# A Fourier mixing block and a gated feed-forward layer on one core: a new order for the first weights' conversions and loads

## The chip, the core and the metric

The kernel runs on one core of one Trainium2 chip. The time is the device time of the core in microseconds. Before the change it is 2035.06 us, the median of three runs (2034.91 to 2035.15). Engines are named as in the profile: PE (TensorE), DVE (VectorE), ACT (ScalarE), POOL (GpSimd) and SP, which only issues DMA transfers here.

## What is computed

The reference, cut to what matters, with x of 8 x 3008 x 256, `w_gate` and `w_val` of 256 x 1536 and `w_out` of 1536 x 256:

```python
X = np.fft.fft(np.fft.fft(x, axis=1), axis=2).real.astype(np.float32)
x = X.reshape(B * S, D)
gate = 1.0 / (1.0 + np.exp(-(x @ w_gate)))
val = x @ w_val
return (gate * val @ w_out).astype(np.float32)
```

`x` comes as float32. The three weights come as float64, 8 bytes a number, and the kernel turns them into float32 on the chip.

## The kernel before, in words

**Weights.** The 18 `jobs` are pieces of weights, 256 x 256 numbers each and 0.52 MB as float64: for each of six column blocks c one piece of the gate (w = 0) and one of the values (w = 1), and one of the output weights (w = 2), which comes one block later. In the order of the list: 0 and 1 are gate and value of block 0, 2 and 3 of block 1, 4 is output block 0, 5 and 6 gate and value of block 2, 7 output block 1, and so on to 17, output block 5. A piece goes through three stages. `weight_load` (L130) issues its DMA from SP into a place `raw`. The conversion is `weight_parts` (L161), two ACT operations (L166, L167), and `weight_join` (L169), three DVE operations (L176, L177, L179) and one POOL addition (L181). `weight_use` (L183) is a `merge` (L190) for gate and value: eight matmuls `ps` that fold the second Fourier transform (over the 256 features, table `dt`) into the weight, two ACT copies into `G2` and `G1` (L197, L198), and two small DMAs that turn one row of `G2` into the columns `ge` (L200). For the output weights it is `forms` (L203): two ACT copies and four POOL subtractions that make seven combinations in `wf`.

The places are borrowed from tiles that the main loop uses later: `raw` and `ws` of pieces 0 to 5 lie in tiles `z`, `pk`, `qk`, `ek`, `ae` and `h`; pieces 6 and 7 in the two tiles `c7`; the pieces from 8 on (`KEEP`) in one tile `mega` of the size of `x4`, which takes the place of the first sequence's input and so can be loaded only when that has been read for the last time.

**First Fourier transform.** Each of the 8 sequences is folded by its symmetries (`fold_ops`, L218), for sequence 0 in two halves on DVE and POOL at the start (L223 to L236), and then multiplied by tables of cosines and sines in `st`. The matmuls `ev` and `od` (`half`, L279) sum over six groups of rows; the four cosine groups of sequence 0 can start with half of the input and the first half of the cosine table, the two sine groups need the sine table. `then` copies one sum out with ACT (L291), and `places` adds and subtracts the other with DVE (L295, L298). The results are `pk`, `qk` and `ek`.

**Main loop.** A sequence's 1505 frequencies go in six chunks of up to 256, each against 12 blocks of 128 hidden features: 12 steps a chunk, 576 steps in all. Step i calls `front` (L343: matmuls `pa` and `pb`, on DVE two `ae` with a column of `ge`, and two `z`), `gate` for the step before (L365: one DVE product `h`, POOL sums `sf`), `back` for two pairs earlier (L388: six or eight matmuls `po`), the conversions' ACT part that is planned for this step (`pre`), the sigmoid (L573), and at last what `side` holds for the step: joins, loads, uses and other planned work. `at(i, f)` puts f into `side`. Every engine carries out its own instructions in the order in which the program gives them (a manual schedule), so a waiting instruction holds what stands behind it on its engine, and a waiting DMA issue holds all later issues of SP. The four PSUM tiles of `psx` are shared by `pa`, `pb`, `ps` and the sums.

**The order around the change.** At the start: loads 0 and 1, `x` of sequence 0, the cosine table, the sine table, loads 2 to 7. Then conversion 0 and merge 0, conversion 1 and merge 1, the fold and the cosine sums, the sine sums; conversions 2 to 5 stand one each ahead of the last four evacuations. `weight_use(2)` and loads 8 to 10 follow. In the first chunk, conversions 6 to 17 are planned by `weight_step` in the steps 1 to 8, two in the odd steps and one in the even ones, each one or two steps ahead of its use; the uses 3 to 17 stand in steps 0 to 9.

Of the kernel before, what the change touches and what calls it, by code (L numbers as in the profile page):

```python
# [7 lines left out]
F32 = mybir.dt.float32  # L8
I32 = mybir.dt.int32
# [36 lines left out]
def kernel(  # L46
# [11 lines left out]
    B, _, _, _, D = xf.shape  # L58
    F = moe_w_gate.shape[1]
    P = 128  # L60
# [6 lines left out]
    NPR = NFT // 2  # L67
    CH = 256
    WC = 256
# [9 lines left out]
    xp = ctx.enter_context(tc.tile_pool(name="xp", bufs=1))  # L79
    pqp = ctx.enter_context(tc.tile_pool(name="pqp", bufs=2))  # L80
    dram = ctx.enter_context(tc.tile_pool(name="dram", bufs=1, space=bass.MemoryType.DRAM))
    evp = ctx.enter_context(tc.tile_pool(name="evp", bufs=2))
    app = ctx.enter_context(tc.tile_pool(name="app", bufs=3))
    zp = ctx.enter_context(tc.tile_pool(name="zp", bufs=3))
    hp = ctx.enter_context(tc.tile_pool(name="hp", bufs=3))
    sp = ctx.enter_context(tc.tile_pool(name="sp", bufs=2))
    cp = ctx.enter_context(tc.tile_pool(name="cp", bufs=2))
    op = ctx.enter_context(tc.tile_pool(name="op", bufs=2))
# [14 lines left out]
    def load_x(b):  # L103
        X[b] = xp.tile([NP, 4, NQ, D], F32, name="x4", tag="x4")
        for h in range(0, 4, 2):
            nc.sync.dma_start(out=X[b][:, h : h + 2], in_=xf[b, :, h : h + 2])
# [11 lines left out]
    def load_table(t, nq):  # L118
        for q in range(0, NQ, nq):
            nc.sync.dma_start(out=st[:, t, q : q + nq], in_=stab[:, t, q : q + nq])  # L120
# [3 lines left out]
    jobs = [(w, c - (w == 2)) for c in range(NPR + 1) for w in range(3)  # L124
            if (c if w == 2 else c < NPR)]
    RAW, WS = {}, {}
    mega = []
    KEEP = 8

    def weight_load(j):  # L130


        w, c = jobs[j]
        src = (moe_w_gate, moe_w_val, moe_w_out)[w]
        src = src[2 * c * P : 2 * (c + 1) * P, :] if w == 2 else src[:, c * WC : (c + 1) * WC]
        src = src.rearrange("(c p) f -> p c f", p=P)
        if j < 6:
            if j < 3:
                raw = zp.tile([P, 2, WC, 2], I32, name="raw", tag="z")
            else:  # L140
                raw = pqp.tile([P, 2, WC, 2], I32, name="raw", tag=("pk", "qk", "ek")[j - 3])
            ws = (app if j < 3 else hp).tile([P, 2, WC], F32, name="ws", tag="ae" if j < 3 else "h")
        else:
            if j < KEEP:
                both = cp.tile([P, 3, 2 * WC], F32, name="both", tag="c7")
                r, i = 0, 2
            else:
                if not mega:
                    mega.append(xp.tile([P, 12, 2 * WC], F32, name="mega", tag="x4"))
                both, r, i = mega[0], (j - KEEP) % 3 * 2, 6 + (j - KEEP) % 6  # L150
            raw = both[:, r : r + 2].rearrange("p a n -> p (a n)").bitcast(I32).rearrange(
                "p (c f w) -> p c f w", c=2, w=2)
            ws = both[:, i].rearrange("p (c f) -> p c f", c=2)
        WS[j] = ws
        if src.dtype == F32:
            nc.sync.dma_start(out=ws, in_=src)
        else:
            RAW[j] = raw
            nc.sync.dma_start(out=raw.rearrange("p c f w -> p c (f w)"), in_=src.bitcast(I32))

    def weight_parts(j):  # L161

        if j in RAW:
            raw, ws = RAW[j], WS[j]
            lo, hi = raw[:, :, :, 0], raw[:, :, :, 1]
            nc.scalar.activation(ws, hi.bitcast(F32), AF.Abs)  # L166
            nc.scalar.activation(lo, lo.bitcast(U32), AF.Copy, scale=2.0 ** -29)  # L167

    def weight_join(j):  # L169
        if j not in RAW:  # L170
            return
        raw, ws = RAW.pop(j), WS[j]
        lo, hi = raw[:, :, :, 0], raw[:, :, :, 1]
        wi = ws.bitcast(I32)
        ts = nc.vector.tensor_scalar
        ts(out=ws, in0=ws, scalar1=2.0 ** -15, scalar2=HUGE, op0=ALU.max, op1=ALU.min)  # L176
        ts(out=wi, in0=wi, scalar1=3, scalar2=0x3FFFFFF8, op0=ALU.logical_shift_left,  # L177
           op1=ALU.bitwise_and)
        nc.vector.scalar_tensor_tensor(out=wi, in0=hi, scalar=-(2 ** 30), in1=wi,  # L179
                                       op0=ALU.bitwise_and, op1=ALU.bitwise_or)  # L180
        nc.gpsimd.tensor_tensor(wi, wi, lo, op=ALU.add)  # L181

    def weight_use(j, other=None):  # L183
        w, c = jobs[j]
        if w == 2:
            forms(WS.pop(j), c)
        else:
            merge(WS.pop(j), w, c, other)

    def merge(ws, g, c, other):  # L190
        cs = slice(c * WC, (c + 1) * WC)
        ps = bank("ps", other)
        for h in range(2):
            for t in range(2):
                mm(ps[:, h * WC : (h + 1) * WC], dt[:, t, h * HD : (h + 1) * HD], ws[:, t, :],
                   h == 0 and t == 0, t == 1)
        nc.scalar.copy(G2[:, g, cs], ps[:, WC : 2 * WC])  # L197
        nc.scalar.copy(G1[:, g, cs], ps[:, 0:WC])  # L198
        for f in range(c * WC // P, (c + 1) * WC // P):
            (nc.sync if c else nc.scalar).dma_start(  # L200
                out=ge[:, g, f : f + 1], in_=G2[0:1, g, f * P : (f + 1) * P])

    def forms(ws, c):  # L203

        w = ws.rearrange("p f (a h j) -> p f h a j", h=2, j=TB)
        f = wf[:, c].rearrange("p m (a j) -> p m a j", j=TB)
        sub = lambda o, a, b: nc.gpsimd.tensor_tensor(o, a, b, op=ALU.subtract)
        nc.scalar.copy(f[:, 0:2], w[:, :, 0])
        nc.scalar.copy(f[:, 2], w[:, 1, 1])
        sub(f[:, 4], w[:, 0, 1], w[:, 0, 0])  # L210
        sub(f[:, 6], w[:, 1, 1], w[:, 0, 1])
        sub(f[:, 5], w[:, 1, 1], f[:, 4])
        sub(f[:, 3], w[:, 1, 0], f[:, 5])
# [92 lines left out]
    def seq_start(b):  # L306
        PQE[b] = (pqp.tile([P, NK], F32, name="pk", tag="pk"),
                  pqp.tile([P, NK], F32, name="qk", tag="qk"),
                  pqp.tile([P, NK], F32, name="ek", tag="ek"))
        if b:  # L310
            nc.sync.dma_start(out=PQE[b][2], in_=ed[b - 1 : b, :].to_broadcast([P, NK]))

    def seq_group(b, blk, what, other=None):
        return half(lambda q: W[b, blk][what][:, q, :], PQE[b][what], blk, what == 1, P, other)
# [163 lines left out]
    for j in range(2):  # L478
        weight_load(j)
    load_x(0)  # L480
    load_table(0, NQ // 2)
    load_table(1, NQ)
    for j in range(2, KEEP):
        weight_load(j)
    for j in range(2):
        weight_parts(j)
        weight_join(j)
        weight_use(j)
    seq_start(0)
    cos = [seq_group(0, blk, what, (2 * blk, 2 * blk + 1) if what else None)  # L490
           for blk in range(2) for what in (0, 2)]
# [4 lines left out]
    sin = [seq_group(0, blk, 1) for blk in range(2)]  # L496
    for sums, _ in sin:
        sums(*range(NQ))
    cos[0][1]()()
    cos[1][1]()()  # L500
    for j, (_, then) in zip(range(2, 6), cos[2:] + sin):
        weight_parts(j)
        weight_join(j)
        then()()
    weight_use(2)
    for j in range(KEEP, KEEP + 3):
        weight_load(j)

    per = 2 * NPR * len(chunks)
    side = {}  # L510

    def at(i, *fs):
        side.setdefault(i, []).extend(fs)
# [2 lines left out]

        at(i, lambda: at(i + 1, f(*args)))

    def weight_step(i, *js):

        for j in js:
            pre.setdefault(i, []).append(lambda j=j: weight_parts(j))
            at(i, lambda j=j: weight_join(j))
            if KEEP <= j < len(jobs) - 3:
                at(i, lambda j=j: weight_load(j + 3))

    pre = {}
    for c in range(1, NPR + 1):
        i, j = 2 * c - 3, 3 * c - 1
        if c < NPR:  # L530
            if c > 1:
                at(i, lambda j=j: weight_use(j))
            at(i + 1, lambda j=j: weight_use(j + 1))
            at(i + 2, lambda j=j: weight_use(j + 2))
        else:
            at(i, lambda j=j: weight_use(j))
        if c == NPR:
            weight_step(i - 1, j)
        elif c > 1:
            weight_step(i - 1, *range(max(j, 6), j + 1))  # L540
            weight_step(i, j + 1, j + 2)
    i0 = 2 * NPR
    at(i0 + 1, lambda: load_x(1), e_load)

# [19 lines left out]
    for i in range(2 * len(pairs)):  # L564
# [7 lines left out]
        z = fresh[2]  # L572
# [63 lines left out]
```

## Time and profile before

| what | us |
|---|---|
| span of the profiled run | 2033.9 |
| busy: PE, DVE, POOL, ACT | 1998.4, 1754.1, 1334.9, 499.2 |
| first matmul of merge 0, of merge 1 | 8.96, 18.79 |
| first cosine sum, first sine sum | 24.41, 39.70 |
| first `pa` of steps 0, 1, 2, 3, 4 | 49.02, 52.47, 55.92, 65.30, 69.76 |
| first `pa` of steps 5, 6, 7, 8, 9 | 77.28, 83.27, 89.47, 95.44, 101.64 |
| idle of PE between 0 and 24.41 | 16.8 |
| idle of PE between 48 and 100 | 9.8 |

The page gives busy times as shares of the span; they are averages over a start, a first chunk with weights in it, and 560 steps without. Times in the text are counted from the start of the span. In a line of the timeline the first number is the start, the second the duration, and the bracket holds the idle time before it and what ended that. In the windows view, each row gives for one stretch the busy time of PE, PEld, DVE, ACT and POOL with the number of instructions, then the granted clock of PE, the share of time that the DMA engines were busy, and GB/s.

### The profile page before, as it was taken

Reading aid. Unit: us, or ns where it says so; the run is one execution under the profiler, and the core shown is the slowest. Engines: PE = TensorE matmul, PEld = TensorE weight load, DVE = VectorE, ACT = ScalarE, POOL = GpSimd, SP = SyncE. Lnnn points to the kernel's source line nnn. Section 1 sums busy time; section 2 is a strip of 40 time slices with the busy share of each in tenths; the row PEclk is TensorE's granted clock in tenths of the full one; section 3 lists DMA queues with packets and bytes.
Section 4 is the critical chain, followed back from the end, with each engine's and each line's share of the span. In section 5 each row is a group of like instructions: output and inputs, shape, how many; then the busy total and the mean of one; then the engine's idle time right before and its main releaser. Section 6 shows DMA issues by size and latency. Waiting matters only on the chain.

```text
span 2033.9 us, 27344 instructions
## 1 busy us (share of the span) xinstructions
PE 1998.4 (98%) x9168; PEld 1740.5 (86%) x9168; DVE 1754.1 (86%) x3221; ACT 499.2 (25%) x875; POOL 1334.9 (66%) x1675
## 2 busy tenths in 40 slices
PE   6899999999999999999999999999999999999998
PEld 4688789888998889888898888988889888898888
DVE  5999778987899878998889978899778988898887
ACT  2522222222222222222222222222222222222222
POOL 3779655875569745696457955589546875565665
PEclk9999999999999999999999999999999999999999
DMA  6340102010021000200011000201002010000001
GB/s 239 104 69 16 27 11 72 18 29 11 11 77 31 11 11 17 76 26 11 15 46 43 26 16 16 72 10 34 14 11 72 15 32 11 11 16 16 11 15 27
DMA packets 136176, 70.98 MB, mean 35 GB/s; under 512 B 127875, under 2 KB 128131, under 8 KB 133642
## 3 DMA queue, kind: packets, MB, share of 16 engines
q1 hardware_dynamic: 134214, 68.69, 12.3%
q8 instruction: 74, 1.21, 0.2%
q10 hardware_dynamic: 1822, 0.54, 0.1%
q14 instruction: 66, 0.54, 0.1%
HBM read 44.50 MB, written 24.68 MB: 34 GB/s over the span
## 4 chain that ended last, share of the span: by engine, by line
PE 86%; DVE 8%; POOL 4%; issue 1%; DMA 0%; ACT 0%; DVEq 0%; ACTq 0%; SPq 0%; POOLq 0%
PE po L93 37%; PE pa L93 21%; PE pb L93 21%; PE ev L93 3%; PE od L93 3%; DVE h L373 2%; DVE ae L358 2%; DVE z L362 1%; POOL x L233 1%; DVE z L361 1%; POOL x L231 1%; PE ps L93 1%; POOL sf L378 1%; DVE os L420 0%; POOL sf L377 0%
## 5 line engine op out<-in xcount | busy, mean ns | idle before, releaser
L573 ACT ACTIVATE z<-z 128x512 f32<-128x512 f32 (+1 forms) x576 | 358.5, 622 | 1311.4 <-DVE z L362 1311.3
L358 DVE SCALAR_TENSOR_TENSOR ae<-ek,ge,pa 128x256 f32<-128x256 f32 (+1 forms) x1152 | 489.8, 466 | 190.8 <-PE pa L93 188.1
L93 PE MATMUL pa<-pk,G 128*128 128x256 f32 (+1 forms) x2304 | 582.5, 375 | 0.0
L93 PE MATMUL pb<-qk,G 128*128 128x256 f32 (+1 forms) x2304 | 581.5, 375 | 0.0
L93 PE MATMUL po<-sf,wf 128*128 128x256 f32 (+1 forms) x2304 | 537.4, 375 | 1.4 <-POOL sf L378 0.7
L93 PEld LDWEIGHTS pa<-pk,G 128*128 128x128 f32 x2304 | 438.1, 190 | 57.2 <-issue 1.3
L93 PEld LDWEIGHTS po<-sf,wf 128*128 128x128 f32 x2304 | 436.2, 190 | 56.5 <-POOL sf L379 4.8
L93 PEld LDWEIGHTS pb<-qk,G 128*128 128x128 f32 x2304 | 438.0, 190 | 49.8
L377 POOL TENSOR_TENSOR sf<-h 128x256 f32<-128x256 f32 (+1 forms) x288 | 212.3, 737 | 391.4 <-DVE h L373 391.4
L373 DVE TENSOR_TENSOR h<-z 128x512 f32<-128x512 f32 (+1 forms) x576 | 453.3, 787 | 0.0
L361 DVE TENSOR_TENSOR z<-ae,pb 128x512 f32<-128x512 f32 (+1 forms) x576 | 390.1, 677 | 61.7 <-DVE ae L358 2.3
L93 PE MATMUL po<-h,wf 128*128 128x256 f32 (+1 forms) x1728 | 412.5, 375 | 0.0
L362 DVE TENSOR_TENSOR z<-ae,pb 128x512 f32<-128x512 f32 (+1 forms) x576 | 386.2, 670 | 0.0
L375 POOL TENSOR_TENSOR sf<-h 128x256 f32<-128x256 f32 (+1 forms) x288 | 220.2, 765 | 217.5 <-DVE h L373 212.6
L93 PEld LDWEIGHTS po<-h,wf 128*128 128x128 f32 x1728 | 328.3, 190 | 37.1
L378 POOL TENSOR_TENSOR sf<-sf,h 128x256 f32<-128x256 f32 (+1 forms) x288 | 216.2, 751 | 22.6
L379 POOL TENSOR_TENSOR sf<-h,sf 128x256 f32<-128x256 f32 (+1 forms) x288 | 214.3, 744 | 22.6
L460 ACT COPY c<-po 128x512 f32<-128x512 f32 (+1 forms) x141 | 76.9, 581 | 63.2 <-PE po L93 63.2
L420 DVE STREAM_TRANSPOSE os<-c 128x256 f32<-128x256 f32 x192 | 84.1, 438 | 0.2
L93 PE MATMUL ev<-st,x 126*128 126x377 f32 (+3 forms) x216 | 75.0, 479 | 1.8 <-DVE x L233 1.8
L93 PE MATMUL od<-st,x 126*128 126x377 f32 (+3 forms) x216 | 74.8, 478 | 0.0
L465 POOL TENSOR_TENSOR c<-c 128x512 f32<-128x512 f32 (+1 forms) x47 | 73.9, 1573 | 0.0
(83 smaller groups left out, 720.7 us busy)
## 6 DMA issues: line engine op xcount, KB each, us to landing
x<-in_xf_dram SPq DMA_DIRECT2D x16, 1512.0 KB
out_dram<-os SPq DMA_DIRECT2D x288, 64.0 KB
ek<-ed SPq DMA_DIRECT2D x7, 752.5 KB
out_dram<-os SPq DMA_DIRECT2D x92, 56.0 KB
st<-in_stab_dram SPq DMA_DIRECT2D x2, 1111.9 KB
st<-in_stab_dram SPq DMA_DIRECT2D x1, 2223.7 KB
mega<-in_moe_w_out_dram SPq DMA_DIRECT2D x4, 512.0 KB
raw<-in_moe_w_gate_dram SPq DMA_DIRECT2D x3, 512.0 KB
```

The source lines that it names most:

```text
L93: nc.tensor.matmul(o, l, r, start=start, stop=stop, skip_group_check=True)
L358: nc.vector.scalar_tensor_tensor(out=ae[:, g], in0=ek[:, ks], scalar=ge[:, g, f : f + 1], in1=pa[:, g], op0=ALU.mult, op1=ALU.add)
L361: nc.vector.tensor_tensor(z[:, :, 0], ae, pb, op=ALU.add)
L362: nc.vector.tensor_tensor(z[:, :, 1, ::-1], ae, pb, op=ALU.subtract)
L373: nc.vector.tensor_tensor(h[:, fh], z[:, 0], z[:, 1], op=ALU.mult)
L375: tt(s[:, 2], h[:, 0, 0], h[:, 0, 1], op=ALU.subtract)
L377: tt(s[:, 0], h[:, 0, 1], h[:, 1, 1], op=ALU.add)
L378: tt(s[:, 1], s[:, 0], h[:, 0, 0], op=ALU.subtract)
L379: tt(s[:, 3], h[:, 1, 0], s[:, 1], op=ALU.subtract)
L420: nc.vector.transpose(os_[:, s, 0:nb, h, :], t[:, slot, 0 : nb * TB])
L460: nc.scalar.copy(t[:, 2 * j : 2 * j + 2, 0:n], PO[j][:, :, 0:n])
L573: nc.scalar.activation(z[:, 0], z[:, 0], AF.Sigmoid)
```

## The change

Four edits. Conversions 0 and 1 both come ahead of merges 0 and 1. Loads 2 to 5 come ahead of the sine table. `KEEP` is 10 in place of 8: pieces 6 and 7 get their `raw` in the tiles `os`, 8 and 9 in the tiles `sf`, and their results in the tiles `c7`. Conversions 2 to 8 are spread over the six evacuations, and those from 9 on stand one a step in steps 0 to 8, with load j+3 behind conversion j. The uses keep their steps, but for the last, which moves from step 9 to step 11. It is to let the first sums start earlier, and to keep merges from waiting for conversions.

```diff
-    KEEP = 8
+    KEEP = 10
...
+        if j < KEEP:
+            pool, tag = ((zp, "z"), (pqp, ("pk", "qk", "ek")[j % 3]), (op, "os"), (sp, "sf"))[
+                j // 3 if j < 6 else j // 2 - 1]
+            raw = pool.tile([P, 2, WC, 2], I32, name="raw", tag=tag)
...
+                ws = some(3, cp, "c7")[:, (j - 6) % 3].rearrange("p (c f) -> p c f", c=2)
...
     load_x(0)
     load_table(0, NQ // 2)
+    for j in range(2, 6):
+        weight_load(j)
     load_table(1, NQ)
-    for j in range(2, KEEP):
+    for j in range(6, KEEP):
         weight_load(j)
-    for j in range(2):
-        weight_parts(j)
-        weight_join(j)
-        weight_use(j)
...
+    weight_parts(0)
+    weight_parts(1)
+    weight_join(0)
+    weight_join(1)
+    weight_use(0)
+    weight_use(1)
...
-    cos[0][1]()()
-    cos[1][1]()()
-    for j, (_, then) in zip(range(2, 6), cos[2:] + sin):
-        weight_parts(j)
-        weight_join(j)
+    evacuate = [then for _, then in cos + sin]
+    for then, js in zip(evacuate, ((2, 3, 4), (5,), (), (), (6, 7), (8,))):
+        weight_round(*js)
         then()()
-    weight_use(2)
     for j in range(KEEP, KEEP + 3):
         weight_load(j)
+    weight_use(2)
...
-        if c == NPR:
-            weight_step(i - 1, j)
-        elif c > 1:
-            weight_step(i - 1, *range(max(j, 6), j + 1))
-            weight_step(i, j + 1, j + 2)
+    for j in range(9, len(jobs)):
+        pre.setdefault(j - 9, []).append(lambda j=j: weight_parts(j))
+        at(j - 9, lambda j=j: weight_join(j))
+        if KEEP <= j < len(jobs) - 3:
+            at(j - 9, lambda j=j: weight_load(j + 3))
+    for j in range(3, len(jobs)):
+        w, c = jobs[j]
+        at(2 * c + (-3, -2, 1)[w], lambda j=j: weight_use(j))
```

More of the change, by code (lines that the diff above doesn't have):

```diff
@@ L126 @@
     RAW, WS = {}, {}
-    mega = []
-    KEEP = 8
+    shared = {}
+    KEEP = 10
     def weight_load(j):
@@ L136, in weight_load, with some @@
         src = src.rearrange("(c p) f -> p c f", p=P)
-        if j < 6:
-            if j < 3:
-                raw = zp.tile([P, 2, WC, 2], I32, name="raw", tag="z")
-            else:
-                raw = pqp.tile([P, 2, WC, 2], I32, name="raw", tag=("pk", "qk", "ek")[j - 3])
-            ws = (app if j < 3 else hp).tile([P, 2, WC], F32, name="ws", tag="ae" if j < 3 else "h")
-        else:
[L144 to L150, printed above, removed]
+        def some(n, pool, tag):
+            key = tag, (j - 6) // 3 if tag == "c7" else 0
+            if key not in shared:
+                shared[key] = pool.tile([P, n, 2 * WC], F32, name=f"w{tag}", tag=tag)
+            return shared[key]
+        if j < KEEP:
+            pool, tag = ((zp, "z"), (pqp, ("pk", "qk", "ek")[j % 3]), (op, "os"), (sp, "sf"))[
+                j // 3 if j < 6 else j // 2 - 1]
+            raw = pool.tile([P, 2, WC, 2], I32, name="raw", tag=tag)
+            if j < 6:
+                pool, tag = ((app, "ae"), (hp, "h"))[j // 3]
+                ws = pool.tile([P, 2, WC], F32, name="ws", tag=tag)
+            else:
+                ws = some(3, cp, "c7")[:, (j - 6) % 3].rearrange("p (c f) -> p c f", c=2)
+        else:
+            both = some(12, xp, "x4")
+            r, i = (j - KEEP) % 3 * 2, 6 + (j - KEEP) % 6
             raw = both[:, r : r + 2].rearrange("p a n -> p (a n)").bitcast(I32).rearrange(
@@ L481, with weight_round @@
     load_table(0, NQ // 2)
+    for j in range(2, 6):
+        weight_load(j)
     load_table(1, NQ)
-    for j in range(2, KEEP):
+    for j in range(6, KEEP):
         weight_load(j)
-    for j in range(2):
-        weight_parts(j)
-        weight_join(j)
-        weight_use(j)
+    def weight_round(*js):
+        for j in js:
+            weight_parts(j)
+            weight_join(j)
+    weight_parts(0)
[4 more added lines that the diff above has]
+    weight_use(1)
     seq_start(0)
@@ L517, in split @@
         at(i, lambda: at(i + 1, f(*args)))
[L519 to L525, printed above, removed]
-    pre = {}
[L528 to L536, printed above, removed]
-        if c == NPR:
-            weight_step(i - 1, j)
-        elif c > 1:
-            weight_step(i - 1, *range(max(j, 6), j + 1))
-            weight_step(i, j + 1, j + 2)
+    pre = {}
+    for j in range(9, len(jobs)):
[6 more added lines that the diff above has]
+        at(2 * c + (-3, -2, 1)[w], lambda j=j: weight_use(j))
     i0 = 2 * NPR
```

## The prediction

> **What bounds the kernel now.** First the page: busy time by engine, and the chain of waits.
>
> ```profile
> PE 1998.4 (98%) x9168; PEld 1740.5 (86%) x9168; DVE 1754.1 (86%) x3221; ACT 499.2 (25%) x875; POOL 1334.9 (66%) x1675
> ...
> PE 86%; DVE 8%; POOL 4%; issue 1%; DMA 0%; ACT 0%; DVEq 0%; ACTq 0%; SPq 0%; POOLq 0%
> ```
>
> TensorE (PE) is busy 1998.4 of 2033.9 us, so all that any reordering can win is 35.5 us of PE idle plus matmuls that ran slowly. Next, PE's waits in three stretches (before 48 us, 48 to 100, after 100) say where that idle time is.
>
> ```profile
> PE ps L93 <- POOL ws L181: 15.0, 2, 9.0
> PE ev L93 <- DVE x L233: 1.8, 1, 1.8
> ...
> PE ps L93 <- POOL mega L181: 5.9, 5, 2.5
> PE ps L93 <- POOL both L181: 3.9, 1, 3.9
> ...
> PE ps L93 <- POOL mega L181: 1.2, 1, 1.2
> PE po L93 <- POOL sf L378: 0.7, 3, 0.3
> ```
>
> 16.8 us lie in the start, 9.8 in the first chunk, 1.9 later; the rest is the tail. Everything but the 1.8 and the 0.7 is a merge (`ps`) waiting for the last operation of a weight conversion (L181). From 101.64 us on PE runs without a break, so what the change moves is the time at which that begins. The timeline of the start:
>
> ```profile
> 8.96 3.78 PE L93 MATMUL ps<-ws,dt 128*128 128x256 f32 x8 [8.96 <-POOL ws L181]
> ...
> 14.43 0.66 ACT L166 ACTIVATE ws<-raw 128x512 f32<-128x512 f32 x1 [1.00 <-ACT G L198]
> ...
> 15.13 0.40 SPq L159 DMA_DIRECT2D raw<-in_moe_w_gate_dram  x1
> ...
> 18.79 3.78 PE L93 MATMUL ps<-ws,dt 128*128 128x256 f32 x8 [6.04 <-POOL ws L181]
> ...
> 24.41 1.53 PE L93 MATMUL ev<-st,x 126*128 126x377 f32 x4 [1.83 <-DVE x L233]
> ```
>
> Conversion 1 starts on ScalarE (ACT) at 14.43, behind merge 0's copies; VectorE's (DVE) fold waits in DVE's order behind it until 16.65, and the first cosine sum behind the fold until 24.41. Then the first chunk by windows (PE, PEld, DVE, ACT, POOL busy, PE clock, DMA share, GB/s):
>
> ```profile
> 57.80:61.70 3.90, 0.01 (x1) 0.00 (x0) 3.73 (x7) 2.06 (x6) 3.82 (x6) 0.85 0.03 0
> 61.70:66.30 4.60, 4.57 (x11) 3.68 (x12) 4.04 (x6) 1.39 (x4) 3.81 (x4) 0.50 0.00 0
> ...
> 72.90:101.60 28.70, 22.76 (x101) 18.76 (x101) 27.73 (x46) 14.04 (x29) 24.15 (x26) 1.00 0.38 111
> ```
>
> From 72.90 to 101.60 DVE is busy 27.73 of 28.70 us and PE only 22.76: **DVE bounds the first chunk**, because twelve conversions share steps 1 to 8 with the chunk's own DVE work. At 61.70 PE also runs at half clock after an idle 3.9 us.
>
> **What the Trainium skill says.** "TensorE: Matmul & The Clock Gate", Part 1, says that an idle window of about 3.4 us halves the clock until about 3.4 us of work have passed. The trace agrees: after 3.91 us idle the eight `ps` matmuls took 3.78 us, after 2.51 us idle only 1.99. "SBUF — State Buffer", Who interferes with whom, says that a DVE instruction with two SBUF inputs, or in a two-port mode, and a GpSimd (POOL) instruction block each other. The trace agrees: L223 took 0.94 us alone and 2.03 with POOL busy, L177 0.43 and 0.84. "DMA: Bandwidth & Descriptors", Anatomy of one DMA, says that a semaphore wait is held by the issuing sequencer. The trace agrees: SP's issue of weight 2 stood 9.0 us for a landing of `x`, and the loads queued after it stood too.
>
> **The change part by part.**
>
> *First two conversions together.* Nothing is removed; ACT no longer puts merge 0's copies (12.78) before conversion 1. Until 15 us the windows sum to 0.5 MB by 4.0 us and 1.34 MB by 6.0, so weight 1 (0.52 MB after weight 0 and the 0.26 MB table) is there at about 6.4. ACT then ends both at 7.7, DVE at about 9.1, POOL at 10.5. Merge 1 follows merge 0 at 12.74 and ends near 15 instead of 22.57. The fold no longer waits for the conversion but for `x`: its first half (4.2 MB cumulative less 1.5) at about 10.6, the second at 15.1 (the issue released at 15.13 waited for it). From L223 at 21.16 to L233's end at 24.36 the chain takes 3.2 us; POOL's 2.52+0.98 us of folding, now at the same time, cost DVE some 2 more (in the trace 16.87 to 21.22 cost it 1.1+1.5). First cosine at 15.1+3.2+2 = 20.3, 4.1 us earlier. But PE has then idled 5 us, so its first 4.5 us go at half clock: 2.2 us back. Cosines (15.1 us) end at 37.6, sines (7.6) at 45.2, DVE's last `qk` 1.1 later: **46.3 instead of 48.56, −2.2 us**.
>
> *Four loads ahead of the sine table.* 2.1 MB go before the table. Cumulative: 6.7 MB up to the cosine table, 8.8 with the four, 11.1 with the sine table; the windows of before reach 11.1 MB at 33.6 us. The table is wanted at 37.6. So it is hidden, unless SP stands: before, weights 3 and 4 waited until 21.26 and 27.56 for `ge` landings. If the table is issued only at 27.6 and 1 MB of weights with it, it lands at 27.6+3.3/0.4+1 = 37; still on time.
>
> *Seven instead of four conversions before the steps.* They move 3 conversions of DVE work into a stage that has DVE idle: 5.2 us in 30 to 40, 1.8 in 40 to 50. Seven at 1.55 (0.43+0.43+0.69) to 2.0 (with the 0.89 form) is 10.9 to 14.0 us, plus six evacuations of 1.09 = 6.5. From the fold's end (29.94 before, about 25.4 after): 25.4+17.4 to 20.5 = 42.8 to 45.9, under the 46.3 above. So they cost nothing there: the sines hide them. The ten places only make this possible.
>
> *One conversion a step, nine in steps 0 to 8.* Their DVE time, from the timeline: 0.41+0.83+1.10 = 2.34 us alone, 2.07 to 2.09 as one of a pair; I take 2.2. The chunk's own DVE work is 0.87+0.69+0.60+0.60 = 2.73 a step. Check on before: 9 steps of `ae`, `z` (19.4) and 8 of `h` (5.2) with 12 conversions (25.7) are 50.3 us, against 49.3 busy between 48.56 and 103.9. After: 24.6+9×2.2 = 44.4 us, 5 less. Idle before was 6.0 us in that stretch: 4.1 for `pa` at the start, after the half clock, and after merges that PE held up while waiting for POOL. Each weight is now converted two to four steps before its use, so those waits go, and with them the half clock. At steps 0 and 1 a conversion fills the gap. I keep 2 us. PE itself needs 9×1.72 (`pa`, `pb`) +5×1.51 (`po`) +9×1.73 (merges) = 38.6 us, less than DVE's, so it doesn't bound.
>
> *A new wait on SP.* The loads of steps 1 to 5 now come before that step's `ge` transfers in SP's order, and wait for POOL's L181 of the same step. Behind them stand the `ge` rows of merges 6 and 9, needed two steps on by `ae` on DVE. From a step's DVE begin: join ends at 5, POOL 6.8, two issues to 7.9, the load's 0.5 MB 1.3 to 2, landing near 11 (before: 2.0 to 2.5 from issue to landing); the need is at 10.2. Not shown by the trace of before; bounds 0 and 2×2 us, I take 1.5. The odd steps have a step more of slack.
>
> First chunk: 44.4+2+1.5 = 47.9 against 55.3, **−7.4**; I shorten it to −6.9, for PE and DVE are close (4.96 and 4.93 a step) once `po` runs. Later work has the same instructions; the last form moves from step 9 to 11, before the load of `x` at step 13. Sum: −2.2−6.9 = −9.1, 2035.1−9.1 = **2026.0 us**.
>
> **The rivals.** *A, both parts in full:* the start keeps its 4.1 us (clock warm) and no `ge` wait: −4.1−8.9 = −13, **2022 us**. For it: merge 1 ends just 5 us before the cosine, and the clock's window is coarse. *B, one part is lost:* no start gain (−6.9), or `ge` stalls of 1.5 us at four even steps, 6 us in place of 1.5 (−4.6): about −5, **2030 us**. For it: SP's longest wait for a `ge` landing was 5.9 us. Against: the windows then had DMA share 0.9, in the chunk 0.38. *C, slower:* the sine table's issue waits for the second pair of `ge` rows. The first pair took 6.3 us apart (21.26, 27.56); at that pace the second pair lands at 34 and 40. Table at 40+2.3/0.4+1 = 46.7, sines to 54.3, `qk` at 55.4, +6.8; weights 6 to 9 land later still and put ACT behind, so that the chunk gains 3, not 7: +4, **2039 us**. Against: 20 us of idle DMA would then shorten those landings.
>
> **How the numbers follow.** Forecast 0.50, A 0.22, B 0.20, C 0.05, 0.03 for none of these within 0.2%. 0.2% is 4.1 us, so faster ends at 2031.0: forecast, A and nearly all of B less a part that falls within, 0.90; same 0.05; slower 0.05. The range takes in A with the unknown waits at nothing (2020.5) and B up to 2031.5.
>
> **What would show it.** Right: `ev` starts at 20 to 21 us, sines end at 44 to 46, no `ps` wait for L181 between 50 and 100, step 9 begins near 92, DVE above 94% busy from step 1 to 8, the tail unchanged in length. Wrong: PE waiting for `st` between 35 and 48 (table late), DVE idle before `ae` for `ge` at steps 4 and 6, or the half clock again inside the chunk.

## The result, and the profile after

| | before | changed |
|---|---|---|
| median of six runs, us | 2035.11 (2034.75 to 2036.59) | 2029.43 (2024.31 to 2032.67) |
| ratio, with 95% interval | | 0.9968 (0.9955 to 0.9982) |
| span of the profiled run, us | 2033.9 | 2028.5 |
| first cosine | 24.41 | 23.85 |
| first `pa` of step 0 | 49.02 | 54.92 |
| first `pa` of step 9 | 101.64 | 96.87 |

The changed kernel is faster by 0.32%, and its times spread over 8.4 us where those of before spread over 1.8. The page of the changed kernel, busy time by engine and the chain of waits:

```profile
PE 1996.6 (98%) x9168; PEld 1743.3 (86%) x9168; DVE 1754.9 (87%) x3221; ACT 498.5 (25%) x875; POOL 1328.4 (65%) x1675
...
PE 85%; DVE 7%; POOL 4%; DMA 2%; issue 1%; ACT 0%; DVEq 0%; SPq 0%; ACTq 0%; POOLq 0%
```

The work is the same. DMA, which had 0% of the chain, now has 2%. PE's waits before 48 us, from 48 to 110, and after:

```profile
PE ev L93 <- DMA st<-in_stab_dram: 11.7, 2, 8.8
PE ps L93 <- POOL ws L187: 9.3, 1, 9.3
...
PE pb L93 <- DVE ae L364: 2.5, 3, 1.5
...
PE po L93 <- POOL sf L384: 0.2, 1, 0.2
```

No merge waits for a conversion any more but the first. (Lines have moved: L176, L177, L179 and L181 of the conversion are L182, L183, L185 and L187, the `ae` of L358 is L364.) In its place PE waits for the tables in `st`. So the whole gain is in the first chunk, and the start lost: from the start of the span to step 0 the changed kernel took 5.9 us more, and steps 0 to 9 took 41.95 us instead of 52.62, 10.7 less; the rest, 0.6 less, makes the 5.4 us between the spans. The start by its timeline:

```profile
9.35 5.76 PE L93 MATMUL ps<-ws,dt 128*128 128x256 f32 x16 [9.35 <-POOL ws L187]
...
18.60 0.95 DVE L229 TENSOR_TENSOR x<-x 126x765 f32<-126x765 f32 x1 [4.26 <-DMA x<-in_xf_dram]
...
22.85 0.56 DVE L239 TENSOR_TENSOR x<-x 126x381 f32<-126x381 f32 x1
...
23.85 2.85 PE L93 MATMUL ev<-st,x 126*128 126x377 f32 x4 [8.75 <-DMA st<-in_stab_dram]
...
29.38 0.46 SPq L120 DMA_DIRECT2D st<-in_stab_dram  x1
...
43.84 3.73 PE L93 MATMUL ev<-st,x 126*128 126x377 f32 x6 [2.92 <-DMA st<-in_stab_dram]
```

Both merges run one after the other and end at 15.1 us, as planned. But the second half of `x` is there only at 18.60, and the part of the fold that PE needs ends at 23.41. PE starts at 23.85, after 8.75 us of standing; what came last for it was not the fold but the first half of the cosine table. The sine table, issued at 29.38, holds PE from 40.9 to 43.84, and the six matmuls after it take 3.73 us, where six at full clock take 2.06: the half clock, a second time. The same stretches of both kernels in the windows view, the changed kernel first:

```profile
12.00:20.00 8.00, 3.10 (x11) 2.24 (x9) 3.31 (x5) 1.29 (x4) 1.53 (x2) 1.00 0.95 295
20.00:28.00 8.00, 4.15 (x8) 2.44 (x9) 7.77 (x13) 0.00 (x0) 2.96 (x3) 0.57 0.92 250
28.00:36.00 8.00, 8.00 (x26) 4.74 (x25) 6.17 (x9) 5.63 (x10) 5.11 (x6) 1.00 0.91 297
```

and the kernel before:

```profile
12.00:20.00 8.00, 1.96 (x5) 1.05 (x5) 4.81 (x6) 1.87 (x4) 3.13 (x2) 0.76 0.94 362
20.00:28.00 8.00, 6.17 (x19) 3.68 (x18) 7.78 (x15) 0.65 (x2) 2.81 (x3) 0.81 0.92 324
28.00:36.00 8.00, 8.00 (x27) 4.81 (x26) 2.95 (x3) 1.64 (x4) 3.73 (x4) 1.00 1.00 365
```

The last two columns are to be seen: the DMA engines were as busy (0.91 to 0.95 against 0.92 to 1.00) but moved 250 to 297 GB/s in place of 324 to 365. The first chunk, steps 0 to 9, of the changed kernel, and then of the kernel before:

```profile
54.70:96.60 41.90, 39.38 (x179) 33.53 (x178) 37.42 (x63) 23.15 (x53) 26.19 (x32) 1.00 0.34 100
```

```profile
48.80:101.40 52.60, 42.75 (x179) 35.29 (x178) 46.98 (x77) 28.51 (x60) 37.18 (x41) 0.94 0.34 101
```

The same 179 matmuls, with 63 DVE instructions instead of 77, 9.6 us less DVE work, and a clock of 1.00 instead of 0.94. Not all of the 9.6 us is saved: some of it only falls after the stretch, because PE is further ahead of DVE at its end than it was before.

### The profile page after: what moved, and what is told of

Its sections match the earlier page's. It is cut to its first block, busy times and chain, and to the rows that moved or that the text cites. A ratio compares the mean times of both kernels' runs of the same rounds, so it can differ in the third digit from the quotient of the medians.

```text
span 2028.5 us, 27347 instructions
## 1 busy us (share of the span) xinstructions
PE 1996.6 (98%) x9168; PEld 1743.3 (86%) x9168; DVE 1754.9 (87%) x3221; ACT 498.5 (25%) x875; POOL 1328.4 (65%) x1675
## 4 chain that ended last, share of the span: by engine, by line
PE 85%; DVE 7%; POOL 4%; DMA 2%; issue 1%; ACT 0%; DVEq 0%; SPq 0%; ACTq 0%; POOLq 0%
PE po L93 37%; PE pa L93 21%; PE pb L93 21%; PE ev L93 3%; PE od L93 3%; DVE ae L364 2%; DVE h L379 2%; DVE z L368 1%; DMA ge<-G 1%; DVE z L367 1%; POOL x L239 1%; POOL x L237 1%; DMA st<-in_stab_dram 1%; POOL sf L384 1%; POOL sf L383 1%
## 5 line engine op out<-in xcount | busy, mean ns | idle before, releaser
L364 DVE SCALAR_TENSOR_TENSOR ae<-ek,ge,pa 128x256 f32<-128x256 f32 (+1 forms) x1152 | 489.7, 466 | 186.1 <-PE pa L93 181.9
```

The source lines that it names most:

```text
L364: nc.vector.scalar_tensor_tensor(out=ae[:, g], in0=ek[:, ks], scalar=ge[:, g, f : f + 1], in1=pa[:, g], op0=ALU.mult, op1=ALU.add)
```

## The experiments

The times of all runs, with the ratio to the kernel before on the same chip and points of the profiled run. Not all rows are from one chip, so it is the ratio that compares them. `qk` is the end of the last DVE operation that makes it.

| run | median us | ratio (95%) | first cosine | `qk` | step 0 | steps 0 to 9 |
|---|---|---|---|---|---|---|
| before_again | 2036.67 | | 25.1 | 51.0 | 51.4 | 51.4 |
| after_again | 2030.79 | 0.9970 (0.9959 to 0.9982) | 23.3 | 53.6 | 54.0 | 42.0 |
| ge_sync | 2029.61 | 0.9971 (0.9958 to 0.9984) | 24.5 | 52.7 | 52.5 | 41.8 |
| table_first | 2029.71 | 0.9968 (0.9956 to 0.9981) | 21.2 | 54.5 | 50.0 | 45.2 |
| merge_first | 2030.29 | 0.9968 (0.9956 to 0.9980) | 25.1 | 53.7 | 54.2 | 41.9 |
| old_start | 2033.20 | 0.9982 (0.9967 to 0.9997) | 24.7 | 54.0 | 50.7 | 44.1 |
| skip_678 | 2029.15 | 0.9961 (0.9947 to 0.9974) | 24.2 | 52.5 | 52.9 | 42.0 |
| split_joins | 2028.87 | 0.9960 (0.9947 to 0.9972) | 25.5 | 54.4 | 54.2 | 40.2 |
| no_table | 2026.58 | 0.9950 (0.9936 to 0.9964) | 24.5 | 51.3 | 51.5 | 42.0 |
| two_ahead | 2031.69 | 0.9977 (0.9968 to 0.9985) | 25.3 | 59.2 | 53.6 | 47.1 |
| chunk_pairs | 2032.01 | 0.9976 (0.9967 to 0.9986) | 24.6 | 54.7 | 54.4 | 43.4 |
| eleven_in_chunk | 2035.84 | 0.9995 (0.9986 to 1.0003) | 25.4 | 54.9 | 54.9 | 47.0 |

From step 9's `pa` to the last `po`, all of these runs and the first two took 1924 to 1926 us, so that the differences lie before step 9. The intervals of the ratios are some 2.5 us to either side: only differences beyond that are settled by the times alone.

**Both kernels once more** (`before_again`, `after_again`). No edit.

> The kernel before, for a second profile. Theory T (in the changed kernel the start now hangs on transfers: x until 18.6 us, the sine table until 43.8): here the transfers are hidden behind merge 1 and the cosines, so whether the DMA moves 350 to 380 GB/s between 12 and 20 us (as in its first profile) or 240 to 300 (as in the profile of the changed kernel), the first cosine starts at 24 to 25.5, step 0 at 49 to 50.5, and the time is 2034.5 to 2037. Rival N (the DMA is slow only because of the changed order): always 350 to 380 GB/s here.

> The changed kernel once more. Theory T: its time follows the DMA's rate in the start: with 350 GB/s or more between 12 and 20 us the first cosine starts at 20 to 21.5, PE waits less than 1 us for the sine table, and the run takes 2026 or less; with under 300 it starts at 23 to 25, PE waits 2 us or more for the table, and it takes 2029 or more. The spread over runs is 5 us or more where that of before is 2. Rival D (DVE's seven conversions set the end of the sines): the spread is not tied to the table, and DVE is busy throughout from 31 to 53 us.

The kernel before, in its second profile, in windows:

```profile
12.00:20.00 8.00, 1.96 (x5) 1.12 (x4) 4.12 (x5) 1.87 (x4) 2.44 (x2) 1.00 0.89 312
20.00:28.00 8.00, 5.94 (x14) 3.71 (x13) 7.81 (x15) 0.65 (x2) 2.85 (x2) 0.88 1.01 296
```

Here the old order moves 312 and 296 GB/s, not 362 and 324, so rival N falls: the rate is in part a matter of the run. Step 0 was 2.4 us later than in the first profile, 0.9 more than T allowed; the time is among those of before on that chip (2035.4 to 2038.1). So the loss at the start depends on the pair of profiles: step 0 of the changed kernel is 5.9 us later in the first pair, 2.6 in this one (54.0 against 51.4), and its steps 0 to 9 are 10.7 and 9.4 us shorter. The changed kernel went by T's branch for a low rate (301 GB/s, a little above T's 300; first cosine at 23.3, 2.7 us of waiting for the table, 2029.7 in that run). Its spread was only 2.5 us, so the spread of 8.4 in the first set was not seen here; that point of T was missed.

**Sine table ahead again** (`table_first`).

```diff
-    for j in range(2, 6):
-        weight_load(j)
     load_table(1, NQ)
-    for j in range(6, KEEP):
+    for j in range(2, KEEP):
         weight_load(j)
```

> The sine table goes ahead of loads 2 to 5 again (this part of the change undone), the rest stays. Theory T: the table lands before 36 us and PE never waits for it; but weights 2 to 4 land 4 to 6 us later and stand on ACT ahead of the evacuation of the first cosine sum, whose PSUM tile the first sine needs, so PE waits there for 0 to 4 us instead; step 0 begins at 47 to 52 against 54.9, the time is 2022 to 2028. Rival D: step 0 not before 54, the time within 1 us of the changed kernel's.

PE's waits before 60 us:

```profile
PE pb L93 <- DVE qk L301: 3.1, 1, 3.1
PE od L93 <- DVE pk L304: 1.6, 1, 1.6
```

The table was never waited for, and step 0's `pa` came at 50.0, as T had it. But weight 2 reached DVE only after DVE had stood 7.7 us, the conversions ran until 53.6, and `pb` waited 3.1 us for `qk`. The evacuation of the first cosine behind weight 4 cost PE 1.6 us, as T had it, `qk` at 54.5 is what D had. The time is that of the changed kernel: T's 2022 to 2028 was missed, D's was right. Before the steps both have to arrive early, the table for PE and the weights for DVE.

**The ge transfers of merges 0 and 1 off the path of the loads** (`ge_sync`).

```diff
-            (nc.sync if c else nc.scalar).dma_start(
+            nc.sync.dma_start(
                 out=ge[:, g, f : f + 1], in_=G2[0:1, g, f * P : (f + 1) * P])
```

> The four ge transfers of merges 0 and 1 are issued by SP behind load 9 instead of by ACT, so that no load at the start waits for their landing. Theory T: loads 4 and 5 and the sine table are issued by 20 us instead of 25.9 to 29.4, the dip of the DMA between 28 and 31 us goes, the table lands 2 to 4 us earlier, and the time falls by 2 to 4 us against the changed kernel (to about 2026). Rival D: the table lands earlier, and the time stays within 1 us.

PE had no wait for the table here, and the dip went (383 GB/s from 28 to 31 us, against 213 in the changed kernel). Step 0 came 1.5 to 2.4 us earlier. The median is 1.2 us lower and the ratio the same, so no gain in the time is shown. SP's own timeline, and the first sine:

```profile
7.27 8.49 SPq L165 DMA_DIRECT2D raw<-in_moe_w_gate_dram  x1
15.80 6.25 SPq L120 DMA_DIRECT2D st<-in_stab_dram  x1
...
43.11 2.14 PE L93 MATMUL ev<-st,x 126*128 126x377 f32 x6
```

The second number is how long the issue itself took, 8.49 and 6.25 us instead of the 0.37 to 0.47 of most others: with some seven transfers under way, an issue stood although nothing that the profile shows was waited for. Loads 4 and 5 were out by 15.8 us, the table only at 22.05. Even so, its issue began 13.6 us earlier than in the changed kernel, and the table did not land earlier: its last landing event in the trace is at 43.02, against 43.70 and 42.81 in the changed kernel's two profiles. T's 2 to 4 us are missed, and a late issue is not what makes the table late. PE came to the sines 2.2 us later than in the changed kernel (first cosine at 24.5, and a longer half clock), so it stood no time before them, and took them at full clock (2.14 us for six matmuls instead of 3.73). That is where step 0 gained.

**The first edit undone alone** (`merge_first`). Conversion 0, merge 0, conversion 1, merge 1, as before.

```diff
-    weight_parts(0)
-    weight_parts(1)
-    weight_join(0)
-    weight_join(1)
-    weight_use(0)
-    weight_use(1)
+    for j in range(2):
+        weight_round(j)
+        weight_use(j)
```

> Only the first edit undone: conversion 1 comes after merge 0 again. Theory T2: with x landing at 17 to 19 us the conversion of weight 1 (over at 16.7) hides in the wait for x, so the first cosine starts within 1.5 us of the changed kernel's 23.3 to 23.9, PE is warmer there (it has just done merge 1), and the time is within 1 us. The prediction's view (the edit brings the first cosine 4.1 us forward): 2 to 4 us slower than the changed kernel.

T2 was right: first cosine 25.1 instead of 23.3 to 23.9, but at full clock, because merge 1 has just been done (the wait before it is 1.8 us); step 0 at 54.2 against 54.0 to 54.9; the same time. The edit that was forecast at 2.2 us shows no gain here. Nor could one show: PE stood before the sines in this run too.

```profile
PE ev L93 <- ACT a L297: 2.5, 1, 2.5
```

The wait is put down to an evacuation, which ended at 43.05; the sine table's last landing event is at 42.92, so without the evacuation PE would have started only 0.1 us sooner.

**Both edits of the start undone** (`old_start`). The diffs of `table_first` and `merge_first` together.

> The changed kernel with both edits of the start undone (conversion 0, merge 0, conversion 1, merge 1; sine table ahead of loads 2 to 5), so seven conversions at the start and one a step remain. Theory T2 (the chunk's new order wins about 10 us of its own, and the start of the change costs because PE gets the table late and DVE its weights late): the first cosine starts at 24 to 25.5, DVE has weight 2 only at 33 or later and is then busy to the end of the start, step 0's pb at 54 to 57, steps 0 to 9 take 41 to 44 us against 51.4 to 52.6 before; the time is 0 to 3 us above the changed kernel's. Rival S (the edits of the start are what is lost, without them all is better): step 0 at 49 to 51 as before, the time 3 to 6 us below the changed kernel's.

DVE waited 11.3 us for weights, weight 2 came at 33.9, `pb` of step 0 at 53.55, steps 0 to 9 took 44.1 us, and the median was 2.4 us above the changed kernel's: near T2 in each number (`pb` came 0.4 us before its range, the steps took 0.1 us more). Rival S's 3 to 6 us less are not in the median. But the intervals overlap, the six times run from 2028.3 to 2038.1 us, and the profile is of the lowest, below the changed kernel's own profile (2028.3 against 2029.7). So this run doesn't settle which start is better, given seven conversions in it.

**Less DVE work at the start** (`skip_678`). As ge_sync, without L182 and L183 of conversions 6 to 8.

```diff
-        ts(out=ws, in0=ws, scalar1=2.0 ** -15, scalar2=HUGE, op0=ALU.max, op1=ALU.min)
...
+        if not 6 <= j <= 8:
+            ts(out=ws, in0=ws, scalar1=2.0 ** -15, scalar2=HUGE, op0=ALU.max, op1=ALU.min)
```

> As ge_sync, but the two tensor_scalar operations of conversions 6, 7 and 8 are left out, so those three pieces of the weights are wrong; it takes 3.3 to 4 us of DVE work out of the start (0.42+0.43, 0.42+1.40, 0.80+0.43). Theory T2 (once the table is no longer late, DVE's conversions set the end of the start): step 0's pb 2.5 to 4 us earlier than in ge_sync (52.9 there), and the time 2 to 4 us below it. If transfers or PE set the end of the start: step 0 and the time within 1 us of ge_sync.

T2 missed: step 0 at 52.9 against 52.5, with the first cosine at 24.2 against 24.5. PE's last sum ended at 51.35 and `qk` 1.1 us later, as soon as DVE can; in ge_sync `qk` came 1.8 us after the sum. So the conversions hold the start up by 0.7 us at most when the weights come in this order. T2's condition, a table no longer late, was not met: PE stood 1.8 us before the sines, with no releaser named in the profile, and started at 43.52, when the table's last landing event (43.43) had come. The times don't settle it alone (medians 0.5 us apart, ratios 0.0010).

**No sine table** (`no_table`). From here on theory X: transfers bind the start.

```diff
-    load_table(1, NQ)
...
-                mm((ev, od)[q % 2], w(q), st[:, int(sn), q, c0 : c0 + n], q < 2, q >= NQ - 2)
+                mm((ev, od)[q % 2], w(q), st[:, 0, q, c0 : c0 + n], q < 2, q >= NQ - 2)
```

> The changed kernel without the load of the sine table (2.28 MB); the sines are taken with the cosine table, so the transform's sine part is wrong, the work on the engines the same. Theory X (with skip_678 missed, the start is bound by transfers: x sets the first cosine, the bytes ahead of the table's end set the sines): no gap and no second half clock of PE near 41 us, sines from 40.5 to 48.5, step 0 at 49.5 to 51.5 instead of 53.8 to 54.7, time 2.5 to 4.5 us below the changed kernel. Rival D (DVE's conversions hold the last qk anyway): step 0's pb not before 53, time within 1.5 us.

PE's waits in this run, up to 130 us:

```profile
PE ev L93 <- DMA st<-in_stab_dram: 10.0, 1, 10.0
PE ps L93 <- POOL ws L187: 9.4, 1, 9.4
PE pb L93 <- DVE ae L364: 2.6, 3, 1.5
```

The wait at 41 us is gone, the one ahead of the first cosine is left, and the small ones of the chunk. Step 0 at 51.5 and 4.2 us less time than the changed kernel are X's; the sines, from 42.2 to 49.9, were 1.4 to 1.7 us later than X had them, and it is the cosine table and not `x` that the profile names for the first cosine. So the table's bytes, with the half clock that they bring, are worth 2.5 to 3.4 us at step 0. The landing events say the same of every kernel here that has loads ahead of the sine table:

| run | last landing of the sine table | first sine |
|---|---|---|
| changed kernel | 43.70 | 43.84 |
| after_again | 42.81 | 42.94 |
| ge_sync | 43.02 | 43.11 |
| merge_first | 42.92 | 43.05 |
| skip_678 | 43.43 | 43.52 |
| split_joins | 44.70 | 44.79 |
| two_ahead | 44.11 | 44.20 |
| chunk_pairs | 44.86 | 45.00 |
| eleven_in_chunk | 45.38 | 45.52 |

Each time the sines begin 0.09 to 0.14 us after the table's last landing, whatever else was changed.

**Two loads ahead of the table in place of four** (`two_ahead`). With ge_sync's edit, and the loads of the chunk behind that step's `ge`.

```diff
-    for j in range(2, 6):
+    for j in range(2, 4):
         weight_load(j)
     load_table(1, NQ)
-    for j in range(6, KEEP):
+    for j in range(4, KEEP):
...
-((2, 3, 4), (5,), (), (), (6, 7), (8,))
+((2, 3), (), (), (4, 5), (6, 7), (8,))
```

> A version meant to be better, from theory X: ge of merges 0 and 1 on SP, in the chunk the loads behind that step's ge transfers, and only loads 2 and 3 ahead of the sine table, 4 and 5 behind it, with the conversions spread (2, 3), none, none, (4, 5), (6, 7), (8) over the evacuations. Theory X: the table lands 1.05 MB, 3 to 3.5 us, earlier than in ge_sync, PE has no gap at 40, step 0 at 50.5 to 52.5, steps 0 to 9 in 40 to 41 us (no ge waits), time 2025 to 2028. Rival D: DVE gets weights 4 to 8 too late, pb of step 0 waits for qk to 54 or later, no gain over ge_sync's 2029.6.

Missed, and rival D holds here: weight 4 came at 45, five conversions were left for the time after it, and `pb` waited 4.1 us for `qk` until 58.8. PE still stood 1.0 us ahead of the sines, for the table: its last landing is at 44.11, later than in ge_sync. The two loads behind it ran beside it; by the end of the table's last packet 3.7 MB of weights had come, as against 3.8 in the changed kernel, so little was taken out of its way.

**Better conversions and the order on SP** (`split_joins`). As ge_sync; the loads behind the uses; for several conversions together, DVE does L182 and L183 of all, then L185 of all (the lines inside `weight_join` are not shown).

```diff
-        if KEEP <= j < len(jobs) - 3:
-            at(j - 9, lambda j=j: weight_load(j + 3))
     for j in range(3, len(jobs)):
         w, c = jobs[j]
         at(2 * c + (-3, -2, 1)[w], lambda j=j: weight_use(j))
+    for j in range(KEEP, len(jobs) - 3):
+        at(j - 9, lambda j=j: weight_load(j + 3))
...
             weight_parts(j)
-            weight_join(j)
+            weight_join(j, 0)
+        for j in js:
+            weight_join(j, 1)
```

> A version meant to be better: as ge_sync, and in the chunk the load of a step stands on SP behind that step's ge transfers, and where several conversions come together at the start DVE does their two tensor_scalar operations (L182, L183) first and their third (L185) after, so that fewer L183 fall on POOL's additions (they took 1.40 instead of 0.43 us there, four times in the profile of the changed kernel). Theory T2: no wait of ae for ge (1.8 us less on DVE), 1 to 2.5 us less at the start: 2 to 4 us below ge_sync's 2029.6 on the same footing, ratio to before 0.9950 to 0.9965. If the start is bound by transfers and not by DVE: no more than 1 us below ge_sync.

The timeline of the changed kernel at step 4, which this takes away (POOL, SP's load, SP's `ge`, and DVE's wait):

```profile
71.06 1.29 POOL L187 TENSOR_TENSOR wx<-wx 128x512 int32<-128x512 int32 x1
...
72.38 0.37 SPq L165 DMA_DIRECT2D wx<-in_moe_w_gate_dram  x1
...
72.85 1.11 SPq L206 DMA_DIRECT2D ge<-G  x2
...
76.56 0.48 DVE L364 SCALAR_TENSOR_TENSOR ae<-ek,ge,pa 128x256 f32<-128x256 f32 x1 [1.34 <-DMA ge<-G]
```

The load goes out when POOL's addition is done, the `ge` rows behind it, and `ae` waits for the second value's row. With the loads behind, DVE has no such wait, and steps 0 to 9 took 40.2 us instead of 41.8: the 1.7 us is shown in the steps, if not in the time. At the start there was no gain (first cosine 25.5, PE without work before it for 10.7 us, the table's landing as late as 44.70), so what the new order of the joins is worth is not shown. The time is 0.7 us below ge_sync's, as the last sentence of the expectation has it for a start bound by transfers. It is the fastest kernel here that leaves nothing out, 0.9960 against 0.9970 of the changed one, with intervals that overlap.

**What won in the chunk** (`chunk_pairs`, `eleven_in_chunk`). First the nine conversions in twos in the odd steps, then eleven conversions instead of nine.

```diff
-        pre.setdefault(j - 9, []).append(lambda j=j: weight_parts(j))
-        at(j - 9, lambda j=j: weight_join(j))
+        i = max(0, (j - 8) // 2 * 2 - 1)
+        pre.setdefault(i, []).append(lambda j=j: weight_parts(j))
+        at(i, lambda j=j: weight_join(j))
...
-            at(j - 9, lambda j=j: weight_load(j + 3))
+            at(i, lambda j=j: weight_load(j + 3))
```

> The changed kernel, but conversions 9 to 17 in the first chunk come as before in twos in the odd steps (9 in step 0, 10 and 11 in step 1, up to 16 and 17 in step 7), with their loads; the uses keep their steps. Theory: what won 10 us in the chunk is that nine conversions are left there and each is done well ahead of its merge, not that they are spread evenly: steps 0 to 9 take 41 to 43.5 us, the time is within 1 us of the changed kernel. Rival E (evenness wins): DVE's long odd steps stop PE, PE waits 3 us or more in steps 1 to 8, steps 0 to 9 take 45 to 49.

```diff
-((2, 3, 4), (5,), (), (), (6, 7), (8,))
+((2, 3, 4), (5,), (), (), (8,), ())
...
-    for j in range(9, len(jobs)):
+    for j in (9, 6, 7, *range(10, len(jobs))):
+        i = max(j - 9, j == 7)
```

> The changed kernel with conversions 6 and 7 moved from the sines back into the first chunk (6 with 9 in step 0, 7 with 10 in step 1, both two steps ahead of their merges); 8 stands alone ahead of the first sine's evacuation. So eleven instead of nine conversions in the chunk, all still ahead of their merges. Theory C (the chunk is bound by its DVE work, so what pays there is the number of conversions moved out): steps 0 to 9 take 4 to 5 us more than the 41.9 of the changed kernel (two conversions of 2.1 to 2.3 us), the start, which transfers bound, is unchanged within 1 us (pb of step 0 at 54 to 56), and the time is 3 to 5 us above the changed kernel's. Rival L (what pays is only that each conversion leads its merge): steps 0 to 9 in 41 to 43, the time within 1 us.

In twos: 43.4 us for steps 0 to 9, so evenness is worth some 1.5 us there, and PE waits 4.5 us for `ae` instead of 2.5, which is a part of what E had, but not its 45 to 49. The time is 1.2 us more, a little over the 1 us allowed, and within the intervals. Eleven: 47.0 us, 5.1 more, the start unchanged (54.9), and 2035.84 us, 5.1 above after_again; its ratio 0.9995 (0.9986 to 1.0003) is clear of 0.9970. PE's waits there up to 130 us:

```profile
PE pb L93 <- DVE ae L364: 4.8, 4, 2.9
PE ev L93 <- DMA st<-in_stab_dram: 2.4, 1, 2.4
```

Two conversions put back cost nearly all of the gain, so rival L falls and theory C holds, each of its numbers at or just over the upper end. PE waits for DVE's `ae`, not for a conversion of its own weight, so it is DVE's work in the chunk that counts. The two stood beside another conversion in their steps, so the 2.5 us for each contains what it costs to have two in a step.

## Why the prediction was right, and where not

The time, 2029.43 against 2026.0, lies in the range, and the direction was right. But that the sum came so near is in part luck: in the first pair of profiles the start missed by 8.1 us and the chunk by 3.8 the other way. The nearest single number is rival B's 2030, which leaves out the gain at the start. By the steps:

*The chunk was right, and sized too low.* Forecast: DVE's stretch from the last `qk` to the end of conversion 17 falls from 55.3 to 47.9 us; it took 47.4 (54.47 to 101.88). The new wait of `ae` for `ge` at steps 4 and 6, taken at 1.5, was 1.3+0.5 = 1.8. The half clock at 60 us went. The term that was mis-sized is what PE gets of this. I carried DVE's 7.4, shortened to 6.9, over to the end. PE's step 9 came 10.7 us sooner after step 0: DVE's 7.9 (55.3 less 47.4), and 2.8 that PE gained on DVE. Before, the `pa` of step 9 was 2.3 us ahead of the end of the last conversion (101.64 and 103.9), because each merge had waited for its conversion; now it is 5.0 us ahead (96.87 and 101.88). From eleven_in_chunk's 2.5 us for each conversion put back, the three that moved out are an estimated 7.6 of the 10.7, rather less if what pairs cost is taken off; that leaves 3 or more for the waits that went and evenness, of which chunk_pairs showed 1.5. (The forecast's 2.73 us of own DVE work a step adds up to 2.76, which weighs nothing here.)

*The start was wrong, by 5 to 8 us: +5.9, in the second pair +2.6, instead of −2.2.* The first step that failed is "the second at 15.1", for the second half of `x`. It came at 18.60. The sum behind it was right, the rate was not: I took the DMA's rate of the one profile of before as the kernel's, and in the thirteen later profiles the engines moved 272 to 342 GB/s between 12 and 20 us instead of 362. The trace shows in what form: this transfer has fourteen landing events, which came between 14.8 and 15.1 in that profile; in the changed kernel ten had come by 16.0, and the last four took until 18.6. In the thirteen later profiles the last came 0.9 to 3.7 us after the first. With it goes a term that the forecast put at nothing without a reason, the landing of the cosine table's first half. It was complete at 23.7, and with `x` in time the first cosine could not have started before that, where the forecast had 20.3. Two terms that followed were right: POOL's folding cost DVE 23.41−18.60−3.2 = 1.6 us (forecast 2), and the half clock took the cosines from 15.1 to 17.1 us (forecast 2.2). The second step that failed is "The table is wanted at 37.6. So it is hidden", with 37 for a late issue. It was wanted at 40.9 and there at 43.7. The forecast summed megabytes at before's rate (11.1 MB by 33.6 us; the changed kernel had 11.1 by 40), left no margin for it, and in that sum took the loads behind the table as waiting for it: some 0.7 MB of loads 6 to 9 came before its end. PE stood 2.9 us, and the half clock took the sines from 7.6 to 9.5, which the forecast had not. no_table shows this as the cause, and ge_sync that an earlier issue would not have helped.

*What stayed a wrong reason even so:* "First two conversions together" was to bring 2.2 us. merge_first shows none: the fold then waits for `x` anyway, what the first cosine gains PE pays in half clock, and with either order PE waits for the sine table afterwards. Seven conversions at the start cost more than the 1.55 to 2.0 us each that I took. In the changed kernel, back to back:

```profile
32.53 1.35 POOL L187 TENSOR_TENSOR ws<-ws,raw 128x512 int32<-128x512 int32 x1 [1.60 <-DVE ws L185]
...
32.77 1.40 DVE L183 TENSOR_SCALAR ws<-ws 128x512 int32<-128x512 int32 x1
```

L183, 0.43 us alone, stands behind POOL's addition for the conversion before, so a conversion took 2.5 us there. The lock that the prediction cites from the Trainium skill's "SBUF — State Buffer", Who interferes with whom, fits these two lines: L183 ends 0.3 us after POOL's addition. It was hidden but for 0.7 us at most, as skip_678 shows. Of the rivals, C named a late table, but put it down to a late issue and at 9 us: the table was late by 3 us, for its bytes, and it took back part of the gain, not all.

**What stays open.** Why the DMA moves 272 to 313 GB/s between 12 and 20 us in the ten profiles that have loads ahead of the sine table, or no such table, and 312 to 362 in the four that have the table first. One of these four, the second of before, is at 312, so the run has a part in it; whether the order has one too was not told apart. Open with it is why some landing events of a transfer come so much later than the others. The spread of the times, 8.4 us in one set of the changed kernel and 2.5 in another, 7.8 in ge_sync and 9.7 in old_start, was not traced in single runs. The mean granted clocks, 0.998 in the fastest and 0.996 in the slowest run of the first set, 0.999 and 0.995 in old_start, suggest that half clock has a part in it; that was not tested.

## What to carry to other kernels

A stage that hides its transfers in one order of work need not hide them in the next: when work moves forward into it, add up the bytes that must land before each first use, with those of loads issued right behind them, and use the lowest rate that more than one profile shows, not the rate of one. Where two engines share a stage, count the work moved out of the engine that bounds it; here each conversion in the first chunk cost some 2.5 us, and an earlier start of PE paid nothing while a table that it needed later was still on its way. Order on an issuing queue is part of the data path: 0.5 MB loads issued ahead of a few small rows cost 1.7 us in steps 0 to 9.

## What the runs showed of the hardware that was not expected

An issue on SP took up to 8.49 us instead of 0.37 to 0.47 with some seven large transfers under way (ge_sync), and a sine table whose issue began 13.6 us earlier landed no earlier (43.02 against 43.70 and 42.81). One transfer's landing events can lie far apart: those of the second half of `x` within 0.3 us in the first profile of before, over 3.1 us in the changed kernel. PE fell to half clock after 2.92 us of idle time at 41 us (clock 0.56 from 44 to 46 us) and, in merge_first, after 2.50 us (0.66 from 45.7 to 48.6 us), while 2.51 us in the kernel before had left it at full clock.
